# Weight load cut in two, first phase reordered, early x load, and state transposed by the DMA in a fused cross-attention and gated-FFN kernel

## The chip, the cores and the metric

One core of a Trainium2 chip runs the whole program. The metric is the device time of one launch in microseconds (us), lower is better. Each kernel ran on the same chip as the kernel before, in alternating rounds, and "faster" or "slower" needs 2%. A variant and the changed kernel mostly ran on different chips. Some executions list a mean granted TensorE clock of 0.985 to 0.993 instead of 0.997 to 1.0. By the medians most kernels took 0.4 to 2 us longer in them (state_pe did not); the experiments give the median of the full-clock executions as well, and where it matters the text says which kind a profile was.

Names: PE is TensorE (matmuls), DVE is VectorE, ACT is ScalarE, POOL is GpSimd, SP is the engine that only issues DMAs ("SPq" is its queue).

## The reference

There are 8 batches of `x` (8 heads, 512 rows, 64 columns) and of `state` (8 heads, 32 rows, 64 columns). Attention is read both ways between them; the two results, 544 rows of 512 columns per batch, go through a gated feed-forward layer with 1536 hidden columns.

```python
scores = scale * np.matmul(x, state.transpose(0, 1, 3, 2))     # scale = 1/8
a = softmax(scores)                                            # over the 32 state rows
xread = np.matmul(a, state)                                    # 512 rows
scores2 = scale * np.matmul(state, x.transpose(0, 1, 3, 2))
sread = np.matmul(softmax(scores2), x)                         # 32 rows
x = np.concatenate([xread, sread], axis=2)                     # heads side by side: 512 columns
gate = np.maximum(x @ w_gate, 0.0)
val = x @ w_val
out = gate * val @ w_out
```

Inputs and outputs are fp32; the kernel computes in bf16.

## The kernel before

The kernel never forms `xread`. It multiplies the state of a batch into the weights first (U = state @ w, small matmuls of 64 rows by 32 columns), then multiplies U by the attention. Four matmuls of 512 columns make a gate/value group (128 hidden columns of one batch), four more an output piece.

The order of everything is by hand. A list, `FIRST`, holds batches 0 and 1 and the start of batch 2; a loop does the rest. Each engine takes its instructions strictly in the order in which the list names them. These steps matter here:

```python
def w_dma(lo, hi, after=None):          # ("w", lo, hi): columns lo..hi of both weights, issued by GpSimd
    for w, src in enumerate((moe_w_gate, moe_w_val)):
        d = nc.gpsimd.dma_start(out=wsb[w][:, :, lo:hi], ...)
        loads["gv"[w], lo] = d.ins.name
        gate(d, after)

def x_dma(b, lo=0, n=H, after=None):    # ("xl", b, head, heads, gate): x of batch b, issued by SP
    d = nc.sync.dma_start(out=xf[b][:, lo:lo + n], in_=x_rows(b, lo, n))
    gate(d, after)                      # after = a load that must have landed first

def st_mm(b0, n):                       # state of n batches transposed by PE: 4 matmuls per batch
    ps = ps_st[b0] = ...
    for k in range(n):
        for par in range(2):
            for half in range(2):
                nc.tensor.matmul(ps[64 * half:64 * half + 64, k], st_b[:, b0 + k, par],
                                 perm[:, par, half]...)

# "u": U piece (columns lo..lo+n);  "ue": its eviction;  "g": gate/value group;  "om": output piece
# "conv": fp32 x to bf16;  "xt", "xe": x transposed by PE, evicted (batches 0 and 1)
# "x_bar": x transposed by the DMA (batch 2 on);  "sc": scores;  "at", "ae": attention transposed, evicted
# "dummy": matmuls on zeros that keep PE busy in stretches that wait
```

The weight stream of the first phase is `("w", 0, 256)`, `("w", 256, 512)`, `("w", 512, 1024)`, `("w", 1024, 1536)`, then three loads of `w_out`. x of batch 2 is held back until the last value columns have landed: `("xl", 2, 0, 8, ("v", 1024))`. States 2 to 7 come in one load, are cast on VectorE and transposed by 24 PE matmuls.

The softmax here doesn't subtract the row's maximum and nothing guards it: scores larger than these inputs give would overflow.

Of the kernel before, what the change touches and what calls it, by code (L numbers as in the profile page):

```python
# [8 lines left out]
FP32 = mybir.dt.float32  # L9
BF16 = mybir.dt.bfloat16  # L10
# [5 lines left out]

FIRST = [
    ("dummy", 9), ("w", 0, 256, ("s", 0)), ("st_cast", 0, 1, "v"), ("st_mm", 0, 1), ("st", 1, 2),
    ("xl", 1, 0, 2, ("x", 0, 4)), ("xl", 1, 2, 2), ("xl", 1, 4, 2), ("xl", 1, 6, 2), ("dummy", 2),
    ("st_ev", 0, 1, "a"), ("conv", 0, 0, 2, "v"), ("xt", 0, 0), ("dummy", 1), ("conv", 0, 2, 2, "v"),  # L20
    ("xe", 0, 0, "a"), ("xt", 0, 1), ("sc", 0, 0, (0,)), ("conv", 0, 4, 2, "v"), ("xe", 0, 1, "a"), ("dummy", 2),
    ("xt", 0, 2), ("exp", 0, 0, 0, 1), ("conv", 0, 6, 2, "v"), ("sc", 0, 0, (1,)), ("dummy", 2), ("xe", 0, 2, "a"),
    ("st_cast", 1, 2, "v"), ("xt", 0, 3), ("sum", 0, 0, 0, 1), ("st_mm", 1, 1), ("exp", 0, 0, 1, 1),
    ("sc", 0, 1, (0,)), ("xe", 0, 3, "a"), ("dummy", 3), ("sum", 0, 0, 1, 1), ("mul", 0, 0, 0, 1, "p"),
    ("st_ev", 1, 1, "a"), ("sc", 0, 1, (1,)), ("dummy", 2), ("w", 256, 512, ("g", 0)), ("exp", 0, 1, 1, 1),
    ("mul", 0, 0, 1, 1, "v"), ("u", 0, 0, 256), ("exp", 0, 1, 0, 1), ("sum", 0, 1, 1, 1), ("u", 1, 0, 256),
    ("ue", 0, 0, 256, 1, "a"), ("sr", 0), ("sum", 0, 1, 0, 1), ("ue", 1, 0, 256, 1, "a"), ("dummy", 4),
    ("conv", 1, 0, 2, "p"), ("ue", 0, 0, 256, 0, "a"), ("mul", 0, 1, 1, 1, "v"), ("mul", 0, 1, 0, 1, "p"),
    ("xt", 1, 0), ("sre", 0), ("dummy", 2), ("ue", 1, 0, 256, 0, "a"), ("conv", 1, 2, 2, "p"), ("at", 0, 0),
    ("conv", 1, 4, 2, "v"), ("at", 0, 1), ("xe", 1, 0, "a"), ("ae", 0, 0, "v"), ("w", 512, 1024), ("xt", 1, 2),  # L30
    ("xt", 1, 1), ("ae", 0, 1, "a"), ("xe", 1, 2, "v"), ("sc", 1, 0, (0,)), ("dummy", 1), ("xe", 1, 1, "v"),
    ("exp", 1, 0, 0, 1), ("sc", 1, 1, (0,)), ("g", 0, 1), ("exp", 1, 1, 0, 1), ("conv", 1, 6, 2, "v"),
    ("w", 1024, 1536), ("gr", 0, 1), ("sum", 1, 1, 0, 1), ("xt", 1, 3), ("sc", 1, 0, (1,)), ("dummy", 4),
    ("xe", 1, 3, "a"), ("gm", 0, 1), ("exp", 1, 0, 1, 1), ("sc", 1, 1, (1,)), ("mul", 1, 1, 0, 1, "p"),
    ("sum", 1, 0, 0, 1), ("exp", 1, 1, 1, 1), ("u", 0, 256, 256), ("wo", 0, 4), ("u", 1, 256, 256),
    ("ue", 0, 256, 256, 0, "a"), ("sum", 1, 1, 1, 1), ("g", 0, 0), ("ue", 0, 256, 256, 1, "a"),
    ("mul", 1, 0, 0, 1, "p"), ("sum", 1, 0, 1, 1), ("gr", 0, 0), ("g", 0, 2), ("mul", 1, 1, 1, 1, "p"),
    ("ue", 1, 256, 256, 1, "v"), ("ue", 1, 256, 256, 0, "a"), ("mul", 1, 0, 1, 1, "p"), ("dummy", 1), ("gm", 0, 0),
    ("gr", 0, 2), ("g", 0, 3), ("wo", 4, 8), ("gm", 0, 2), ("gr", 0, 3), ("at", 1, 1), ("wo", 8, 12), ("at", 1, 0),
    ("gm", 0, 3), ("ae", 1, 1, "a"), ("sr", 1), ("ae", 1, 0, "a"), ("u", 0, 512, 256), ("sre", 1), ("u", 0, 768, 256),  # L40
    ("ue", 0, 512, 256, 0, "a"), ("ue", 0, 512, 256, 1, "v"), ("g", 1, 1), ("ue", 0, 768, 256, 0, "a"),
    ("ue", 0, 768, 256, 1, "v"), ("g", 0, 5), ("gr", 1, 1), ("gr", 0, 5), ("gm", 1, 1), ("g", 0, 6), ("gm", 0, 5),
    ("gr", 0, 6), ("g", 0, 7), ("gm", 0, 6), ("xl", 2, 0, 8, ("v", 1024)), ("gr", 0, 7), ("st", 2, 8), ("g", 1, 3),
    ("gm", 0, 7), ("gr", 1, 3), ("u", 0, 1280, 256), ("gm", 1, 3), ("g", 0, 4), ("ue", 0, 1280, 256, 0, "a"),
    ("gr", 0, 4), ("ue", 0, 1280, 256, 1, "v"), ("g", 1, 2), ("gm", 0, 4), ("gr", 1, 2), ("u", 0, 1024, 256),
    ("g", 0, 11), ("gm", 1, 2), ("ue", 0, 1024, 256, 0, "a"), ("gr", 0, 11), ("ue", 0, 1024, 256, 1, "v"),
    ("g", 0, 10), ("gm", 0, 11), ("gr", 0, 10), ("g", 0, 8), ("gm", 0, 10), ("gr", 0, 8), ("g", 0, 9), ("gm", 0, 8),
    ("gr", 0, 9), ("u", 1, 1024, 256), ("g", 1, 0), ("gm", 0, 9), ("ue", 1, 1024, 256, 1, "a"),
    ("ue", 1, 1024, 256, 0, "a"), ("u", 1, 512, 256), ("gr", 1, 0), ("om",), ("ue", 1, 512, 256, 0, "v"),
    ("ue", 1, 512, 256, 1, "a"), ("gm", 1, 0), ("g", 1, 9), ("gr", 1, 9), ("g", 1, 8), ("gm", 1, 9), ("gr", 1, 8),  # L50
    ("u", 1, 1280, 256), ("om",), ("gm", 1, 8), ("ue", 1, 1280, 256, 1, "a"), ("ue", 1, 1280, 256, 0, "a"),
    ("xb_alloc", 2), ("conv", 2, 0, 4, "v"), ("conv", 2, 4, 4, "p"), ("om",), ("g", 1, 11), ("xc", 2, 0, 2, "v"),
    ("xc", 2, 2, 2, "p"), ("at_alloc", 2), ("x_bar", 2), ("xl", 3, 0, 8), ("oe",), ("st_cast", 2, 8, "v"),
    ("gr", 1, 11), ("g", 1, 10), ("gm", 1, 11), ("gr", 1, 10), ("st_mm", 6, 2), ("gm", 1, 10), ("st_mm", 4, 2),
    ("st_ev", 6, 2, "a"), ("st_mm", 2, 2), ("st_ev", 4, 2, "v"), ("u", 1, 768, 256), ("st_ev", 2, 2, "a"), ("om",),
    ("ue", 1, 768, 256, 1, "v"), ("ue", 1, 768, 256, 0, "a"), ("u_alloc", 2), ("u", 2, 512, 512),
    ("ue", 2, 512, 512, 0, "a"), ("ue", 2, 512, 512, 1, "v"), ("sc", 2, 1), ("sc", 2, 0), ("ue", 2, 512, 512, 3, "a"),
    ("om",), ("ue", 2, 512, 512, 2, "v"), ("exp", 2, 1), ("om",), ("exp", 2, 0), ("sum", 2, 1), ("u", 2, 1024, 512),
    ("xb_alloc", 3), ("conv", 3, 4, 4, "p"), ("oe",), ("ue", 2, 1024, 512, 0, "a"), ("sr", 2),
    ("ue", 2, 1024, 512, 3, "a"), ("om",), ("mul", 2, 1, 0, 2, "p"), ("sum", 2, 0), ("ue", 2, 1024, 512, 2, "a"),  # L60
    ("om",), ("sre", 2), ("mul", 2, 0, 0, 2, "p"), ("ue", 2, 1024, 512, 1, "a"), ("conv", 3, 0, 4, "v"), ("g", 1, 7),
    ("a_bar", 2), ("xc", 3, 0, 2, "v"), ("xc", 3, 2, 2, "p"), ("at_alloc", 3), ("x_bar", 3), ("xl", 4), ("gr", 1, 7),
    ("g", 1, 6), ("gm", 1, 7), ("gr", 1, 6), ("g", 1, 5), ("gm", 1, 6), ("gr", 1, 5), ("g", 1, 4), ("gm", 1, 5),
    ("gr", 1, 4), ("om",), ("gm", 1, 4), ("u", 2, 0, 512), ("oe",), ("ue", 2, 0, 512, 0, "v"), ("om",),
    ("ue", 2, 0, 512, 2, "a"), ("ue", 2, 0, 512, 1, "v"), ("ue", 2, 0, 512, 3, "a"), ("om",), ("om",), ("oe",),
]

@with_exitstack
def kernel(
# [9 lines left out]
    nc = tc.nc  # L79

    B, H, S, D = x.shape
# [8 lines left out]
    def pool(name, bufs, space=None):  # L90
        if space is None:
            return ctx.enter_context(tc.tile_pool(name=name, bufs=bufs))
        return ctx.enter_context(tc.tile_pool(name=name, bufs=bufs, space=space))

    const = pool("const", 1)
# [14 lines left out]
    id128 = const.tile([128, 128], BF16, name="id128")  # L110
    perm = const.tile([128, 2, 2, NJ, 64], BF16, name="perm")
    xs_all = [const.tile([128, NC, NJ, 132], BF16, name="xs%d" % i) for i in range(3)]
    warm = const.tile([128, 512], BF16, name="warm")
    st_f = const.tile([128, B, 2, D], FP32, name="st_f")
    st_b = const.tile([128, B, 2, D], BF16, name="st_b")
    stT = const.tile([128, B, NJ, 64], BF16, name="stT")
    brT = const.tile([128, B, NJ * Ns], BF16, name="brT")
    tiny = const.tile([128, 1], FP32, name="tiny")
# [4 lines left out]
    def cp(eng, o, i):  # L123
        if eng == "a":
            nc.scalar.copy(out=o, in_=i)  # L125
        elif eng == "v":
            nc.vector.tensor_copy(out=o, in_=i)  # L127
        else:
            nc.gpsimd.tensor_copy(out=o, in_=i)  # L129
# [4 lines left out]
    def gate(d, after):  # L134
        if after is not None:
            info = mybir.DependencyInfo(mybir.DependencyClass.Sync, mybir.DependencyReason.DATA)
            tc.add_manual_dep(d.ins, loads[after], info, reason="order of loads")

    def st_dma(lo, hi, after=None):
        src = state.rearrange("b h (m t) d -> (h m) b (t d)", t=2)[:, lo:hi]  # L140
        d = nc.sync.dma_start(out=st_f[:, lo:hi].rearrange("p b t d -> p b (t d)"), in_=src)
        loads["s", lo] = d.ins.name
        gate(d, after)

# [42 lines left out]

    def st_ev(b0, n, eng):
        cp(eng, stT[:, b0:b0 + n].rearrange("p b j c -> p (b j c)"), ps_st[b0].rearrange("p b c -> p (b c)"))



# [262 lines left out]

    nc.vector.memset(warm, 0.0)  # L456
    make_identity(nc, id128)
    st_dma(0, 1)
    for j in range(NJ):
        x_dma(0, 2 * j, 2)  # L460
# [5 lines left out]
    for i in range(3):  # L466
        set_ones(i)

    steps = {
        "dummy": dummies, "w": w_dma, "wo": wo_dma, "st": st_dma,  # L470
        "st_cast": st_cast, "st_mm": st_mm, "st_ev": st_ev, "conv": x_conv, "xc": x_copy, "xt": x_tr, "xe": x_ev,
        "sc": sc_mm, "exp": sc_exp, "sum": nrm_sum, "mul": nrm_mul, "at": a_tr, "ae": a_ev,
        "u": u_mm, "ue": u_ev, "g": gv_mm, "gr": gv_relu, "gm": gv_mult, "gv": gv, "om": out_mm, "oe": out_ev, "sr": sr_mm, "sre": sr_ev, "out": outp,
        "xb_alloc": xb_alloc, "at_alloc": at_alloc, "u_alloc": u_alloc, "x_bar": x_bar, "a_bar": a_bar, "ub": u_burst, "xl": x_dma,
# [94 lines left out]
```

## Time and profile before

| | |
|---|---|
| time | 227.07 us (median of 3, 226.51 to 227.14) |
| span in the profile | 224.4 us |
| PE busy | 96% of the span |
| PE's one long wait | 1.78 us, ends at 22.65 us, on value weights 512 to 1023 |
| from 22.65 us to the first gate/value group of batch 2 (57.68 us) | 35.03 us |
| from there to the end of the span | 166.7 us |

The head of the page names each engine's busy time, its share of the span and its instruction count:

```profile
span 224.4 us, 4881 instructions
...
PE 214.4 (96%) x1947; PEld 106.1 (47%) x1969; DVE 140.0 (62%) x246; ACT 117.3 (52%) x218; POOL 37.2 (17%) x47
```

PE is 96% busy in 224.4 us, so the kernel can become shorter only by a few waits at the start or by less PE work. The prediction below shows where these are. SP's timeline (start, duration of the issue, instruction) shows when x of batch 2 was asked for, and when its transpose was:

```profile
27.32 0.38 SPq L151 DMA_DIRECT2D xf<-in_x_dram  x1
...
40.02 1.35 SPq L238 DMA_TRANSPOSE xT<-xb  x1
```

By the tile's view the transpose needed 4.8 us to land, so it was there at 44.8 us, and the scores of batch 2 that read it started at 45.15 us. The slack of that chain was about 0.3 us. The last value weights landed at 27.3 us (the x load is held for them and went out at 27.32) and PE asked for them at 27.52 us: a slack of 0.2 us.

VectorE's timeline shows the same conversion of x (two heads, fp32 to bf16) at two prices. The first is of batch 0, with GpSimd idle; the second of batch 1, with GpSimd converting and issuing a load next to it:

```profile
4.95 0.43 DVE L127 CAST xs<-xf 128x512 bf16<-128x512 f32 x1
...
12.33 0.81 DVE L127 CAST xs<-xf 128x512 bf16<-128x512 f32 x1 [0.70 <-DMA xf<-in_x_dram]
```

### The profile page before, as it was taken

The numbers are of one execution on the slowest core, as the hardware profiler recorded it, in microseconds if no ns is written. First come the engines' busy times: TensorE is split into PE (matmuls) and PEld (weight loads), VectorE is DVE, ScalarE is ACT, GpSimd is POOL, SyncE is SP. The second block draws the span as 40 slices with busy tenths as digits, with TensorE's granted clock in tenths as the row PEclk, the third lists the DMA queues.
The fourth block names the chain that finished last, engine by engine and source line by source line (L and its number), as shares of the span: only waits on it lengthen the run. The fifth ranks groups of instructions, "written<-read, shape, count | busy, mean of one in ns | idle before, by whom it ended". The sixth has DMA issues, their size and how long they took to land.

```text
span 224.4 us, 4881 instructions
## 1 busy us (share of the span) xinstructions
PE 214.4 (96%) x1947; PEld 106.1 (47%) x1969; DVE 140.0 (62%) x246; ACT 117.3 (52%) x218; POOL 37.2 (17%) x47
## 2 busy tenths in 40 slices
PE   6887999999999999999999999999999999999994
PEld 3553444444544444444444444444444444586543
DVE  4777796888377657866595659564956544452210
ACT  3787777676373646363745465455636344343111
POOL 4496001225070160007000700000000000000000
PEclk9999999999999999999999999999999999999999
DMA  6999998674944851385119611361131111111133
GB/s 181 262 201 206 204 226 238 112 265 79 218 183 101 243 132 47 67 267 134 55 33 283 121 47 50 93 146 50 47 93 57 47 47 50 47 48 38 59 80 107
DMA packets 40551, 27.84 MB, mean 124 GB/s; under 512 B 21200, under 2 KB 36304, under 8 KB 40528
## 3 DMA queue, kind: packets, MB, share of 16 engines
q1 hardware_dynamic: 34720, 22.81, 36.6%
q0 software_dynamic: 5808, 4.72, 13.6%
q8 instruction: 15, 0.25, 0.5%
q14 instruction: 8, 0.07, 0.1%
HBM read 18.35 MB, written 8.91 MB: 121 GB/s over the span
## 4 chain that ended last, share of the span: by engine, by line
PE 88%; DMA 6%; POOL 2%; SPq 1%; issue 1%; DVE 0%; ACT 0%; POOLq 0%
PE o_ps L400 38%; PE gv_ps L363 36%; PE u_ps L311 5%; PE gvs_ps L385 5%; DMA wv_sb<-in_moe_w_val_dram 4%; DMA st_f<-in_state_dram 2%; PE sc_ps L246 1%; PE o_ps L425 1%; PE sr_ps L292 1%; SPq L151 1%; POOL wg_sb L157 1%; PE stT_ps L184 1%; POOL xs L129 1%; POOL a_sn L269 1%; POOL wv_sb L157 0%
## 5 line engine op out<-in xcount | busy, mean ns | idle before, releaser
L372 DVE TENSOR_TENSOR h_sb<-gv_ps,g_sb 128x512 bf16<-128x512 f32 x96 | 65.5, 689 | 48.7 <-ACT g_sb L369 48.2
L363 PE MATMUL gv_ps<-ans,U 128*128 128x512 bf16 x384 | 94.3, 379 | 0.1
L400 PE MATMUL o_ps<-wo_sb,h_sb 128*128 128x512 bf16 x350 | 91.3, 379 | 1.4 <-issue 0.5
L369 ACT ACTIVATE g_sb<-gv_ps 128x512 bf16<-128x512 f32 x96 | 57.4, 598 | 55.1 <-PE gv_ps L363 54.3
L363 PEld LDWEIGHTS <-U 128*128 128x128 bf16 x384 | 36.4, 98 | 42.5 <-issue 1.0
L400 PEld LDWEIGHTS <-h_sb 128*128 128x128 bf16 x372 | 35.1, 98 | 43.1 <-issue 4.2
L125 ACT CAST U<-u_ps 128x512 bf16<-128x512 f32 x55 | 29.2, 596 | 5.1 <-PE u_ps L311 4.5
L127 DVE CAST U<-u_ps 128x512 bf16<-128x512 f32 x41 | 25.7, 673 | 3.7 <-PE u_ps L311 3.5
L129 POOL CAST xb<-xf 128x1024 bf16<-128x1024 f32 x10 | 10.2, 1043 | 83.8 <-PE gv_ps L363 38.2
L125 ACT COPY o_sb<-o_ps 128x512 f32<-128x512 f32 (+2 forms) x20 | 10.8, 538 | 19.2 <-PE o_ps L400 17.5
L127 DVE COPY o_sb<-o_ps 128x512 f32<-128x512 f32 (+2 forms) x18 | 11.4, 636 | 9.9 <-ACT o_sb L125 4.5
L257 ACT ACTIVATE e_sn<-sc_ps 128x512 bf16<-128x512 f32 (+1 forms) x20 | 10.1, 514 | 9.9 <-PE sc_ps L246 9.7
L311 PE MATMUL u_ps<-wv_sb,stT 64*32 64x256 bf16 (+1 forms) x280 | 9.6, 309 | 2.2 <-DMA wv_sb<-in_moe_w_val_dram 2.2
L389 DVE TENSOR_TENSOR hs_sb<-gvs_ps,g_sb 128x256 bf16<-128x256 f32 x12 | 5.1, 424 | 9.9 <-ACT g_sb L388 9.9
L263 DVE TENSOR_REDUCE cs<-e_sn 128x8 f32<-128x256 bf16 (+2 forms) x15 | 10.6, 708 | 0.5 <-ACT e_sn L257 0.3
L129 POOL COPY xs<-xb 128x1024 bf16<-128x1024 bf16 x10 | 10.4, 1065 | 1.0 <-DVE xb L127 0.7
L311 PEld LDWEIGHTS <-stT 64*32 64x32 bf16 x560 | 5.9, 90 | 9.8 <-issue 8.0
L311 PE MATMUL u_ps<-wg_sb,stT 64*32 64x256 bf16 (+1 forms) x280 | 10.0, 315 | 0.0
L388 ACT ACTIVATE g_sb<-gvs_ps 128x256 bf16<-128x256 f32 x12 | 4.6, 384 | 10.2 <-PE gvs_ps L385 7.8
L454 PE MATMUL warm_ps<-warm 128*128 128x256 bf16 x33 | 6.7, 321 | 1.2 <-DVE warm L456 1.2
L246 PEld LDWEIGHTS <-xT 128*128 128x128 bf16 x128 | 5.8, 98 | 4.2 <-ACT xT L125 0.7
L246 PE MATMUL sc_ps<-stT,xT 128*128 128x64 bf16 x128 | 6.9, 193 | 0.4
(48 smaller groups left out, 109.6 us busy)
## 6 DMA issues: line engine op xcount, KB each, us to landing
out_dram<-o_sb SPq DMA_DIRECT2D x31, 256.0 KB, 2.4
xf<-in_x_dram SPq DMA_DIRECT2D x6, 1024.0 KB, 6.7
xf<-in_x_dram SPq DMA_DIRECT2D x8, 256.0 KB, 4.8
wo_sb<-in_moe_w_out_dram POOLq DMA_DIRECT2D x3, 512.0 KB, 14.1
wg_sb<-in_moe_w_gate_dram POOLq DMA_DIRECT2D x2, 512.0 KB, 8.0
wv_sb<-in_moe_w_val_dram POOLq DMA_DIRECT2D x2, 512.0 KB, 10.6
wg_sb<-in_moe_w_gate_dram POOLq DMA_DIRECT2D x2, 256.0 KB, 5.4
wv_sb<-in_moe_w_val_dram POOLq DMA_DIRECT2D x2, 256.0 KB, 5.8
```

The lines of the kernel that those rows point to most:

```text
L125: nc.scalar.copy(out=o, in_=i)
L127: nc.vector.tensor_copy(out=o, in_=i)
L129: nc.gpsimd.tensor_copy(out=o, in_=i)
L246: nc.tensor.matmul(ps_sc[b, kc][:, c, :, j2], xT[b][:, c, j], stT[:, b, j].rearrange("p (s n) -> p s n", s=2), start=True, stop=True)
L257: nc.scalar.activation(out=esl(e_sn, b, kc, j2, n).rearrange("p k j n -> p k (j n)"), in_=ps_sc[b, kc].rearrange("p c s j n -> p (c s) j n ...
L263: nc.vector.reduce_sum(out=c, in_=e, axis=AX.X)
L311: nc.tensor.matmul(ps[32 * j:32 * j + 32, 0:n], stT[r, b, j, 32 * kc:32 * kc + 32], wsb[w][r, j, lo:lo + n], start=(i == 0), stop=True, sk ...
L363: nc.tensor.matmul(ps.rearrange("p (c t) -> p c t", c=NC), U[b][:, kc, w, f0:f0 + 128], ANS[b][:, :, kc], start=(kc == 0), stop=(kc == 1))
L369: nc.scalar.activation(out=g_sbs[b, jf], in_=ps_g[b, jf][0], func=AF.Relu)
L372: nc.vector.tensor_tensor(out=hsb[b][:, jf], in0=ps_g[b, jf][1], in1=g_sbs[b, jf], op=ALU.mult)
L385: nc.tensor.matmul(ps[:, w].rearrange("p (b n) -> p b n", b=B), wsb[w][:, j, f0:f0 + 128], brT[:, :, 32 * j:32 * j + 32], start=(j == 0), ...
L400: nc.tensor.matmul(o_ps[0], src[:, jf, t0:t0 + 128], wo_sb[:, jf], start=(jf == 0), stop=(jf == NF - 1))
```

## The change

The intent: let PE work through the arrival of the weights without the 1.78 us wait, and take the state transposes of batches 3 to 7 off PE. Its four parts, cut to their core:

```diff
 FIRST = [                                    # (reordered throughout; only the marked steps here)
-    ("w", 512, 1024)                         # after the evictions of batch 0's attention
+    ("w", 512, 768)                          # right behind ("w", 256, 512)
+    ("w", 768, 1024)
-    ("xl", 2, 0, 8, ("v", 1024))             # x of batch 2 held for the last value weights
+    ("xl", 2, 0, 8, ("v", 768))              # ... for columns 768 to 1023
-    ("st", 2, 8), ("st_cast", 2, 8, "v"), ("st_mm", 6, 2), ("st_mm", 4, 2), ("st_mm", 2, 2)
+    ("st", 2, 3), ("st_cast", 2, 3, "v"), ("st_mm", 2, 1)
+    ("st", 3, 8), ("st_z", 0, "p"), ("st_z", 1, "v"), ("st_z", 3, "v"), ("st_z", 2, "a"), ("st_bar",)
 ]
+    sz_f = const.tile([128, B - 3, 2, D], FP32, name="sz_f")
+    sz_b = const.tile([128, B - 3, 2, 2, D], BF16, name="sz_b")
...
+    def st_z(r, eng):
+        p = slice(32 * r, 32 * r + 32)
+        cp(eng, sz_b[p, :, :, r % 2], sz_f[p])
+
+    def st_bar():
+        nc.sync.dma_start_transpose(out=stT[:, 3:B].rearrange("p b (g j) c -> p (b g) (j c)", g=2),
+                                    in_=sz_b.rearrange("p b g s d -> p (b g s d)"))
...
+    nc.gpsimd.memset(sz_b, 0.0)
```

`st_z` copies 32 rows of one head into the half of a zeroed tile that this head owns, so that one DMA transpose ("the crossbar") gives the layout that the PE matmuls gave before. The gate/value order is the part that the short diff cannot show. Ahead of the first U piece from the last weight columns (1280 to 1535) the list before has nine gate/value groups; the changed list has twelve, because it takes the work of *both* batches on the columns that are there before it asks for new ones:

```text
before:   (0,1) (0,0) (0,2) (0,3) (1,1) (0,5) (0,6) (0,7) (1,3)                     then U of columns 1280
changed:  (0,1) (0,0) (0,3) (0,2) (0,5) (1,1) (1,0) (0,4) (1,4) (1,5) (0,7) (0,6)   then U of columns 1280
          (batch, group of 128 columns)
```

## The prediction

> **What bounds the kernel now.** I read the slices of the page first, then PE's timeline, then what PE waited for.
>
> ```profile
> PE   6887999999999999999999999999999999999994
> DMA  6999998674944851385119611361131111111133
> ```
>
> One digit is a fortieth of 224.4 us, so 5.6 us. From the fifth slice on PE (TensorE) is full to the end; in slices 2 to 6 the DMA engines are full too. So only the first 23 us or so are not bound by PE's own work: there the weights arrive. The list of PE's waits agrees:
>
> ```profile
> PE u_ps L311 <- DMA wv_sb<-in_moe_w_val_dram: 2.2, 2, 1.8
> ...
> PE o_ps L400 <- issue: 0.5, 3, 0.2
> ```
>
> The long wait is in PE's timeline (start, duration, instruction, count):
>
> ```profile
> 18.79 1.03 PE L363 MATMUL gv_ps<-ans,U 128*128 128x512 bf16 x4
> 19.66 0.61 PE L274 MATMUL aT_ps<-id,a_sn 128*128 128x128 bf16 x8
> 20.20 0.43 PE L292 MATMUL sr_ps<-xs,e_sn 128*32 128x65 bf16 x32
> 20.56 0.30 PE L311 MATMUL u_ps<-wg_sb,stT 64*32 64x256 bf16 x8
> 22.65 0.30 PE L311 MATMUL u_ps<-wv_sb,stT 64*32 64x256 bf16 x8 [1.78 <-DMA wv_sb<-in_moe_w_val_dram]
> 22.76 0.30 PE L311 MATMUL u_ps<-wg_sb,stT 64*32 64x256 bf16 x8
> 22.86 0.30 PE L311 MATMUL u_ps<-wv_sb,stT 64*32 64x256 bf16 x8
> 23.10 4.49 PE L363 MATMUL gv_ps<-ans,U 128*128 128x512 bf16 x20
> 27.52 0.30 PE L311 MATMUL u_ps<-wg_sb,stT 64*32 64x256 bf16 x8
> 27.64 0.29 PE L311 MATMUL u_ps<-wv_sb,stT 64*32 64x256 bf16 x8
> 27.87 1.90 PE L363 MATMUL gv_ps<-ans,U 128*128 128x512 bf16 x8
> ...
> 41.85 1.50 PE L184 MATMUL stT_ps<-perm,st_b 128*64 128x256 bf16 x24
> 43.28 0.30 PE L311 MATMUL u_ps<-wg_sb,stT 64*32 64x256 bf16 x8
> ```
>
> What to see: at 20.56 the order demands U from columns 512 to 767, but they come in one load of 512 columns and land at 22.65, though gate and value work of batch 1 on columns 0 to 511 was ready to run. From 22.65 PE never stops again. Whatever changes the end must bring useful PE work before that point, or take PE work away after it.
>
> Unit costs, from differences of starts, since durations overlap: a gate/value or output group of four 512-column matmuls 0.8625 us (16 of them from 50.11 to 53.56 is 3.45). Eight U matmuls of 256 columns 0.11 us, so a 256-column U piece (16) 0.22, a 512-column one 0.43. From 23.10 to 27.87 there are 20 x 0.2156 = 4.31 of full matmuls and one U piece of 0.22; 0.24 is left over, the price of going into the 64*32 mode and out again. The 24 state matmuls take 43.28 - 41.85 = 1.43.
>
> **What the Trainium skill says.** "TensorEngine Tiling (Array Packing)", section Key Properties: changing the tiling mode drains TensorE. The trace agrees: about 0.12 us a switch, by the sum above. "DMA: Bandwidth & Descriptors", section Queues, rings and completion order: each DMA engine goes round robin between the queue rows that have work, packet by packet. The trace agrees in kind: in stretches of 2 us the weight queue moved 0.40 to 0.41 MB alone (16 to 24 us), but 0.32, 0.24 and 0.16 MB from 30, 32 and 34 us, while the x queue took 0.13, 0.24 and 0.42. The same page, section DMA Transpose (X-bar), lets 2-byte data be transposed by the DMA from SP: here an xT transpose of sixteen 128x128 blocks lands in 4.5 us (median).
>
> **The change part by part.** Both first phases hold 24 gate/value groups, 15 U pieces and 12 output pieces; the loop behind is unchanged. So I compare the start of batch 2's gate/value work: 57.68 us before.
>
> *Earlier stream.* The load of columns 512 to 1023 is cut in two, and 512 to 767 is issued right behind 256 to 511. The stream was already busy, so bytes do not come faster: columns to 1023 landed at 22.6, those to 511 at about 15.6, so 767 should land near 19. GpSimd pays two more issues at 0.77 us. Its queue, by durations of before: first multiply ends about 8.8; four issues to 11.9; convert 0.65, multiply 0.63, convert 0.65 to 13.8; four issues to 16.9; two multiplies of 512 columns at 1.34 (2.69 for two at 50.13) to 19.6.
>
> *New order of PE.* The last x pair of batch 1 is converted at 13.8; transpose, copy, scores put gate/value (0,1) at about 15.0 (14.23 before). Then 0.86, U 0.46, state read 0.4, three groups 2.6: 19.4; U of columns 512 is then there. The transposes of batch 1's attention wait for the multiply at 19.6; with the state matmuls of batch 2 (0.24) and another U piece, gate/value (0,5) starts at about 21.0. My estimate from single durations.
>
> *What is left from there.* 20 gate/value 17.25; 12 output 10.35; seven 256-column U 1.54; three 512-column U 1.29; scores of batch 2 0.48; state read 0.36; nine excursions into other modes at 0.235, 2.1. Sum 33.4, so 54.4. The same sum for before from 22.65: rest of the U pieces 0.45, 17.25, 10.35, six U 1.32, three 1.29, state matmuls 1.43, 0.36, 0.48, nine excursions 2.1, two switches inside an excursion 0.24: 35.3, against 35.03 seen. So the account holds to 0.3.
>
> 57.68 - 54.4 gives 3.3 us: 1.65 from starting 1.65 earlier (21.0 for 22.65) and the rest, some 1.65, from less work. Of that, state matmuls are 1.43: 20 fewer in all, about 1.2, and four that moved ahead. The count of mode switches hardly falls (33 changes of mode in the new first phase, 32 in the old): I give that part of the title almost nothing.
>
> *Off the path.* The crossbar for states 3 to 7 replaces PE work, a 1.40 us VectorE cast and three copies of 0.6 to 0.7 by four row copies and ten transposed blocks (estimate from 4.5 us for sixteen: 3 us). It is needed only by scores of batch 3, at about 56. Four more dummy matmuls lie in stretches that wait anyway. The memset of the padded state lies in GpSimd's idle time of 1.60 us before the first weights.
>
> **The rivals.** (1) *The early x load delays the weights.* x of batch 2 is now released by columns 768 to 1023 (about 22.6) and not by the last columns (27.3). The last weights landed at 27.3 without it. In the trace x of batch 2, issued at 27.3, moved little before 30 and needed 10.9 us. Issued at 22.6 it would take from about 25 on a fifth to a third of the stream and put the last columns at 28.5 to 29.9 (estimate from the 2 us stretches). PE wants them at 21.0 + 3.45 + 0.46 + 1.73 + 0.46 + 1.73 = 28.8. So a wait of 0 to 1 us, mean perhaps 0.4: a gain of 2.9, or 2.3 at the bad end. (2) *The front is slower than I think.* GpSimd's chain carries more issues; each 0.3 us of slip in a multiply or conversion goes straight to PE. 0.3 to 1 us more lost. (3) *The state's copies block an in-order engine.* The load of states 3 to 7 is queued on SP behind the x transposes of batch 2, so goes out at about 36 and lands near 42 (estimate); VectorE reaches its copies at about 42.5. A late landing stops VectorE and then, PSUM full, PE. There is about 2 us of slack in PSUM buffers, so I expect nothing; badly, 2 us and a gain of 1. (4) *Output weights late.* x takes from their stream too, but the total of bytes until 38 us is no larger; third output piece at about 39.4. Nothing. (5) *More gain than the sum:* only if PE's front end starts before 21.0; the x and weight landings leave at most half a microsecond: 4 us in all.
>
> **Range and chances.** 3.3 from the sum, less 0.4 for the shared stream and a further 0.1 for slips: 2.8 us. The time is then 227.07 - 2.8 = 224.3. The good end is 4 us and a bit (222.8), the bad end rivals 1 to 3 together (226.2). The line for faster is 222.5, 4.5 us: beyond what the account offers, 0.08. Slower than 231.6 needs a broken tail: 0.02. Within 2%: 0.90.
>
> **What would show it.** Right: PE's wait for the value weights before columns 512 gone; gate/value (0,5) of batch 0 near 21.0; batch 2's gate/value starts near 54.5 to 55; the state group of 24 gone from the timeline; the steady loop unchanged to 0.3 us. Wrong: a wait of over 1 us at the U piece of columns 1280 (rival 1), PE idle before the attention transposes at 19 to 21 (rival 2), VectorE idle on the state load near 42 (rival 3), or a wait of scores of batch 3 for a transpose. If batch 2 starts at 54.5 and the end does not follow, my claim that the rest is unchanged is wrong.

## The result

The changed kernel took 224.77 us (median of 4 runs, 224.15 to 225.06); the kernel before, in the same rounds, 227.10 us (226.51 to 228.21). A ratio in this document is the mean time of one kernel's runs over that of the other's of the same rounds, so not quite the ratio of the medians: here 0.9888, with a 95% interval of 0.9845 to 0.9932. That is 1.1% faster, "same" by the 2% line. Outputs are correct.

The page of the changed kernel, head and two rows of the slices (one digit is a fortieth of the span, in tenths busy):

```profile
span 222.4 us, 4870 instructions
...
PE 215.7 (97%) x1953; PEld 105.2 (47%) x1953; DVE 141.1 (63%) x245; ACT 114.4 (51%) x212; POOL 41.8 (19%) x51
...
PE   6979999999999999999999999999999999999994
...
DMA  6999998979936831576138811351131111111133
```

PE is full one slice sooner: the seven in the fourth slice before (16.8 to 22.4 us) is a nine. (PE's busy time rises by 1.3 us although it has less to do. Matmul records can be missing from a trace; the steady loop's output matmuls count 372 after and 350 before for the same work. So I compare starts of instructions, not busy sums.)

PE's waits (engine, line, releaser: total us, times, longest):

```profile
PE xT_ps L246 <- DVE xs L128: 1.3, 3, 0.6
...
PE xT_ps L246 <- POOL xs L130: 0.6, 1, 0.6
...
PE sc_ps L260 <- DMA xT<-xb: 0.2, 1, 0.2
```

No wait for weights is left. In its place stand waits for *conversions of x* in the first 14 us, and a small one for a transposed x much later. PE's timeline shows where (start, duration, instruction, count, idle time before it):

```profile
12.77 0.40 PE L246 MATMUL xT_ps<-id,xs 128*128 128x128 bf16 x4 [0.61 <-POOL xs L130]
13.65 0.40 PE L246 MATMUL xT_ps<-id,xs 128*128 128x128 bf16 x4 [0.49 <-DVE xs L128]
...
14.80 0.39 PE L246 MATMUL xT_ps<-id,xs 128*128 128x128 bf16 x4
...
15.84 1.03 PE L377 MATMUL gv_ps<-ans,U 128*128 128x512 bf16 x4
...
20.24 0.30 PE L325 MATMUL u_ps<-wg_sb,stT 64*32 64x256 bf16 x8
20.36 0.29 PE L325 MATMUL u_ps<-wv_sb,stT 64*32 64x256 bf16 x8
...
21.82 3.63 PE L377 MATMUL gv_ps<-ans,U 128*128 128x512 bf16 x16
...
29.72 0.30 PE L325 MATMUL u_ps<-wg_sb,stT 64*32 64x256 bf16 x8
29.84 0.29 PE L325 MATMUL u_ps<-wv_sb,stT 64*32 64x256 bf16 x8
...
55.38 1.04 PE L377 MATMUL gv_ps<-ans,U 128*128 128x512 bf16 x4
...
57.43 0.41 PE L260 MATMUL sc_ps<-stT,xT 128*128 128x64 bf16 x8 [0.15 <-DMA xT<-xb]
```

Read it from the top. U of columns 512 (20.24, 20.36) runs without a pause, since value columns 512 to 767 landed at 19.3 us. Group (0,5) of batch 0 starts at 21.82. U of the last columns (29.72, 29.84) runs without a pause too: these weights landed at 28.3 us. Batch 2 starts at 55.38, 2.30 us sooner than before. At 57.43 the scores of batch 3 wait 0.15 us for a transposed x. The rest of the span takes 222.4 - 55.38 = 167.0 us, against 166.7 before: that is unchanged to 0.3.

The conversions behind the first two waits, in VectorE's timeline:

```profile
6.94 0.43 DVE L128 CAST xs<-xf 128x512 bf16<-128x512 f32 x1 [0.48 <-DMA xf<-in_x_dram]
...
12.43 1.16 DVE L128 CAST xs<-xf 128x512 bf16<-128x512 f32 x1 [0.51 <-DMA xf<-in_x_dram]
```

The same instruction takes 0.43 us for batch 0 and 1.16 us for batch 1, where GpSimd runs a conversion (12.06 to 12.71), a multiply (12.64 to 13.30) and another conversion (13.21 to 14.06).

How x of batch 2 shares the DMA engines is seen in two stretches of 2 us, 22 to 24 and 30 to 32 us (queue: packets, MB, share; q0 is the weight queue, q1 that of SP with x):

```profile
q0 software_dynamic: 374, 0.37, 111.0%
q1 hardware_dynamic: 160, 0.03, 14.3%
...
q0 software_dynamic: 242, 0.24, 70.0%
q1 hardware_dynamic: 242, 0.25, 45.2%
```

x was asked for at 21.99 us and hardly moved at first (its queue took 0.03 MB from 22 to 24); from 26 us on it took half of the bytes. It landed at 35.6 us, 13.6 us after it was asked for and 2.6 us sooner than before (38.2).

### The profile page after: what moved, and what is told of

It is laid out like the page before. It is cut to its first block, busy times and chain, and to the rows that moved or that the text cites. A ratio compares the mean times of both kernels' runs of the same rounds, so it can differ in the third digit from the quotient of the medians.

```text
span 222.4 us, 4870 instructions
## 1 busy us (share of the span) xinstructions
PE 215.7 (97%) x1953; PEld 105.2 (47%) x1953; DVE 141.1 (63%) x245; ACT 114.4 (51%) x212; POOL 41.8 (19%) x51
## 4 chain that ended last, share of the span: by engine, by line
PE 89%; DMA 7%; DVE 1%; SPq 1%; issue 0%; ACT 0%
PE o_ps L414 38%; PE gv_ps L377 37%; PE u_ps L325 6%; PE gvs_ps L399 5%; DMA xf<-in_x_dram 4%; DMA xT<-xb 2%; PE sc_ps L260 1%; PE o_ps L439 1%; PE sr_ps L306 1%; SPq L156 1%; PE aT_ps L288 1%; DVE xs L128 1%; DVE U L128 0%; DVE ans L128 0%; SPq L142 0%
## 5 line engine op out<-in xcount | busy, mean ns | idle before, releaser
L414 PE MATMUL o_ps<-wo_sb,h_sb 128*128 128x512 bf16 x372 | 94.1, 379 | 0.0
L383 ACT ACTIVATE g_sb<-gv_ps 128x512 bf16<-128x512 f32 x96 | 57.3, 597 | 54.5 <-PE gv_ps L377 53.9
L126 ACT CAST U<-u_ps 128x512 bf16<-128x512 f32 x52 | 27.7, 595 | 5.8 <-PE u_ps L325 5.2
L128 DVE CAST U<-u_ps 128x512 bf16<-128x512 f32 x44 | 27.7, 674 | 0.8 <-PE u_ps L325 0.8
L130 POOL CAST xb<-xf 128x1024 bf16<-128x1024 f32 x11 | 11.2, 1040 | 71.3 <-DMA xf<-in_x_dram 71.3
L130 POOL COPY xs<-xb 128x1024 bf16<-128x1024 bf16 x11 | 11.2, 1042 | 1.0 <-DVE xb L128 0.7
L277 DVE TENSOR_REDUCE cs<-e_sn 128x32 f32<-128x1024 bf16 (+2 forms) x13 | 10.4, 801 | 0.4 <-ACT e_sn L271 0.2
```

The source lines that it names most:

```text
L126: nc.scalar.copy(out=o, in_=i)
L128: nc.vector.tensor_copy(out=o, in_=i)
L130: nc.gpsimd.tensor_copy(out=o, in_=i)
L277: nc.vector.reduce_sum(out=c, in_=e, axis=AX.X)
L383: nc.scalar.activation(out=g_sbs[b, jf], in_=ps_g[b, jf][0], func=AF.Relu)
L414: nc.tensor.matmul(o_ps[0], src[:, jf, t0:t0 + 128], wo_sb[:, jf], start=(jf == 0), stop=(jf == NF - 1))
```

## The experiments

Twelve runs in three calls; the kernel before ran in each (medians 226.99, 227.57 and 227.08 us). All kernels gave correct results.

| run | what it is | time (us) | ratio to before | 95% | full-clock runs: median (of 6) | before, the same |
|---|---|---|---|---|---|---|
| changed_again | the changed kernel, unaltered | 224.58 | 0.9880 | 0.9842 to 0.9918 | 224.56 (5) | 227.15 |
| one_load | changed, columns 512 to 1023 in one load | 225.54 | 0.9919 | 0.9874 to 0.9964 | 225.23 (4) | 226.97 |
| unpaired | changed, nine groups ahead of columns 1280 | 225.18 | 0.9899 | 0.9874 to 0.9925 | 225.19 (6) | 227.06 |
| x_late | changed, x of batch 2 behind the last weights | 228.05 | 1.0025 | 0.9976 to 1.0075 | 227.84 (1) | 226.97 |
| state_pe | changed, states 3 to 7 by PE | 227.01 | 0.9979 | 0.9938 to 1.0021 | 227.20 (5) | 226.97 |
| state_pe2 | the same, with the memset kept | 226.02 | 0.9954 | 0.9917 to 0.9991 | 225.78 (5) | 227.06 |
| warm | changed, nine more dummies | 225.01 | 0.9883 | 0.9849 to 0.9917 | 225.01 (6) | 227.15 |
| conv_act | changed, one x conversion on ScalarE | 226.04 | 0.9952 | 0.9920 to 0.9984 | 225.60 (5) | 227.06 |
| b_split_move | before, load split, one U piece moved | 227.11 | 1.0003 | 0.9953 to 1.0053 | 226.97 (5) | 226.97 |
| b_front | the same, mended | 227.65 | 0.9996 | 0.9963 to 1.0029 | 227.50 (5) | 227.15 |
| b_xbar | before, with the crossbar alone | 227.99 | 1.0048 | 1.0004 to 1.0091 | 227.36 (3) | 227.06 |
| b_front_xbar | before, with both | 228.30 | 1.0013 | 0.9974 to 1.0053 | 228.21 (5) | 227.15 |

The ratios and their intervals use all executions. Three of the profiles are at 0.992, and in each the low clock is one stretch of some 4 us, with 1.00 around it, that begins at or just behind PE's waits for data: in conv_act the mean granted clock is 0.83, 0.50 and 0.81 in 8 to 10, 10 to 12 and 12 to 14 us (waits of 0.77 and 0.84 us just before), in b_front 0.96, 0.50 and 0.68 in 10 to 12, 12 to 14 and 14 to 16 us (waits of 0.82 and 1.09 us), in b_front_xbar 0.50 and 0.66 in 30 to 32 and 32 to 34 us (a wait of 2.16 us).

My theory: 1.7 us of the gain is the wait at 22.65 us, 1.3 us is PE work that went to the crossbar, each worth its amount alone. The rival: the parts depend on each other, and one of them alone gives little, since something else binds just behind.

### Taking one part out of the changed kernel

**one_load.** The load of columns 512 to 1023 is joined again.

```diff
-    ("w", 512, 768), ...  ("w", 768, 1024), ...  ("xl", 2, 0, 8, ("v", 768)),
+    ("w", 512, 1024), ...                        ("xl", 2, 0, 8, ("v", 512)),
```

> The changed kernel, but columns 512 to 1023 of both weights in one load each again, issued where the load of 512 to 767 is, and x of batch 2 released by it. My theory (the split is what lets PE go on at 20.2 us): the U piece of columns 512 waits for the whole load, until about 22.0 where columns 768 to 1023 landed in the changed kernel, so a wait of 1.5 to 1.8 us comes back at that piece and the time is 226.3 to 226.6. Rival (the bytes are the same and only the order of the work matters; the split is worth nothing): no wait there, 224.8 within 0.4.

Measured 225.54 us. The wait came back where it had been:

```profile
21.82 0.30 PE L325 MATMUL u_ps<-wv_sb,stT 64*32 64x256 bf16 x8 [1.01 <-DMA wv_sb<-in_moe_w_val_dram]
```

It is 1.0 us and not the 1.5 to 1.8 I expected, and the time lies between the two expectations: some 0.8 us above the changed kernel, which is not clear of noise (the intervals overlap). The profile is clearer: from gate/value (0,1) to (0,5) it took 7.35 us (15.94 to 23.29) against 5.98 in both profiles of the changed kernel. So the split takes 1.4 us off PE's path in this order.

**unpaired.** The changed kernel with nine gate/value groups ahead of the last columns instead of twelve, so the old way of asking for new columns early. The groups and U pieces behind stand in another order too; the loads, the states and x are as in the changed kernel.

```diff
-    ... ("g", 1, 5), ("u", 1, 768, 256), ("g", 0, 7), ("g", 0, 6), ("u", 0, 1280, 256), ...
+    ... ("u", 0, 1280, 256), ("g", 0, 7), ("g", 0, 6), ("g", 1, 5), ...     (evictions moved along)
```

> The changed kernel, but the U piece of columns 1280 is asked for after one group of batch 1 on columns 512 to 1023 and not after four gate/value groups and a U piece more; those groups come later. Theory (the gain of the new order is that both batches' work on the columns at hand lies before the demand for the next; the stream is the bound up to 28.3): demand at about 26.5, the last columns land at 28.3 to 28.6, so a wait of 1.6 to 2.1 and 226.2 to 226.9. Rival (once the load is split, any order of these groups does): no wait over 0.3, 224.6 to 225.

Measured 225.18 us. The wait for the last weights is there:

```profile
28.55 0.30 PE L325 MATMUL u_ps<-wv_sb,stT 64*32 64x256 bf16 x8 [1.13 <-DMA wv_sb<-in_moe_w_val_dram]
```

Its direction is as expected, its size half. From (0,5) to batch 2 it took 34.55 us instead of 33.23 (changed_again). The time rose by 0.4 to 0.6 us only, because in this profile (0,5) started 0.2 us sooner and the tail behind batch 2's start was 166.6 us instead of 167.1. A difference of that size is not clear of noise, so what this run shows is the wait in its trace: the order of twelve groups is what hides the late landing of the last weights.

**x_late.** x of batch 2 held for the last weights, as before the change.

```diff
-    ("xl", 2, 0, 8, ("v", 768)),
+    ("xl", 2, 0, 8, ("v", 1024)),
```

> The changed kernel, but x of batch 2 released by the last weight columns again (about 28 us for 22). My theory (the early x load is no gain in itself but the new order, which has taken batch 2's scores forward, needs it): x lands near 38.5 in place of 35.6, its two conversions end near 40.6, the transposed x comes near 46, PE waits 2 to 4 us around the first scores of batch 2 at 42.9: 227 to 228.5. Rival (it only shares the stream, so without it the weights come sooner and nothing waits): 224.8 within 0.4 or a little faster.

Measured 228.05 us: the whole gain is gone, as expected. x was asked for at 28.02 us and landed 10.9 us later at 38.9, 3.3 us after the changed kernel's; its transpose was asked for at 41.04 and needed 5.2 us; PE stood:

```profile
46.33 0.41 PE L260 MATMUL sc_ps<-stT,xT 128*128 128x64 bf16 x8 [1.64 <-DMA xT<-xb]
```

From (0,5) to batch 2 it took 35.92 us, 2.7 more than in changed_again; most of what the wait leaves of that is in two sets of U pieces that were held by evictions (1.30 and 1.09 us for what took 0.85). Five of the six executions were at the lower clock, so the loss in the table has some of that in it; the one at full clock took 227.84 us. In the new order PE asks for the scores of batch 2 at 42.88 us; the transposed x of the changed kernel lands at 37.73 + 5.0 = 42.7.

**state_pe and state_pe2.** States 3 to 7 loaded, cast and transposed by 20 PE matmuls again, at the place where the changed list has them ready. state_pe drops the memset too; state_pe2 keeps one of the same bytes, since the first profile had a slow start.

```diff
-    ("st_z", 0, "p"), ("st_z", 1, "v"), ... ("st_z", 3, "v"), ... ("st_z", 2, "a"), ... ("st_bar",),
+    ("st_cast", 3, 8, "v"), ... ("st_mm", 3, 2), ("st_mm", 5, 2), ("st_mm", 7, 1), ("st_ev", 3, 2, "a"), ...
-    nc.gpsimd.memset(sz_b, 0.0)
+    nc.gpsimd.memset(pad, 0.0)       # twice; in state_pe2 alone
```

> The changed kernel, but states 3 to 7 are transposed by PE again: one cast by VectorE and 20 state matmuls in one excursion after the output pieces at about 51.4 us, no crossbar. My theory (PE never rests there, so its work is time): 20 times 0.06 plus one excursion of 0.24 is 1.4, less at most 0.2 that PE now waits for the transposed x of batch 3: 226.0 to 226.2. Rival (the crossbar and its copies cost about what they save, through waits of VectorE and a busy transpose queue): 224.8 within 0.4.

> States 3 to 7 by PE in the changed order, as before, but with GpSimd's early memset kept at its old cost (two of 640 columns on an unused buffer), so that the front is that of the changed kernel. From gate/value (0,5) to batch 2's gate/value took 33.2 to 33.6 us in the changed kernel's two profiles and 34.55 in the first try. Theory (the state work costs PE 1.3 and the crossbar gives back up to 0.6; the rest of the first try's 2.4 was a slower front, by luck of the load of x or by the missing memset): that stretch 34.3 to 34.6 again, time 225.5 to 226.3. Rival (PE state work costs the full 2.4): 226.8 to 227.3 with a front no later than the changed kernel's 22.5.

state_pe measured 227.01 us, more than I expected. Its profile has (0,5) at 23.60 us; the profiled front was 1.1 us later than that of changed_again (22.48), with half-rate matmuls and a late load of x. state_pe2 measured 226.02 us, inside its expectation and 1.25 to 1.44 us above the changed kernel (224.77, 224.58). In both, (0,5) to batch 2 takes 34.55 us, 1.32 more than in changed_again, and here is the difference:

```profile
52.74 1.28 PE L188 MATMUL stT_ps<-perm,st_b 128*64 128x256 bf16 x20
```

It runs from 52.74 to the next group at 53.95: 1.21 us, as the prediction had it (1.2 for 20). So in the new order the crossbar gives about its full PE time in this stretch: 1.32 us against changed_again, 1.0 against the first profile of the changed kernel (33.56). The front stays open: in state_pe2's profile too (0,5) came late, at 23.33 us, although the memset was kept. In both, a conversion of batch 1's x on VectorE took 1.5 to 1.6 us beside GpSimd's work.

### Adding one part to the kernel before

**b_split_move.** The load is split, and U of columns 768 goes behind two groups that don't need it.

```diff
-    ("w", 512, 1024),
+    ("w", 512, 768), ("w", 768, 1024),
-    ("u", 0, 512, 256), ("u", 0, 768, 256), ... ("g", 1, 1), ("g", 0, 5), ...
+    ("u", 0, 512, 256), ... ("g", 1, 1), ("g", 0, 5), ("u", 0, 768, 256), ...
```

> The kernel before, with only the load of columns 512 to 1023 cut in two at its old place, and the U piece of columns 768 moved behind gate/value (1,1) and (0,5). State on PE and late x as before. My theory (the wait of 1.8 us at 20.6 is a matter of which columns are asked for): U of columns 512 goes at about 20.6, the two gate/value groups fill the time to 22.6, the wait falls to under 0.3: 225.3 to 225.6. Rival (the new order of the whole front is what removes it, and with the old order GpSimd's two more issues push the multiplies back): 226.5 to 227.5.

Measured 227.11 us, ratio 1.0003: a miss. No wait for weights stands at 20.6 us any more. Two new ones do:

```profile
21.03 0.62 PE L274 MATMUL aT_ps<-id,a_sn 128*128 128x128 bf16 x8 [0.73 <-POOL a_sn L269]
```

One is for a multiply on GpSimd, which now stands behind two more load issues of 0.75 to 0.8 us each; the other, 0.68 us at 25.49, for the eviction of a U piece that is used right after it is made. This is my edit's fault, not the old order's, so I mended it.

**b_front.** As b_split_move, with the first `w_out` issue behind the four multiplies and one more group ahead of the use of the late U piece.

```diff
-    ("u", 0, 256, 256), ("wo", 0, 4), ... ("mul", 1, 0, 1, 1, "p"), ("dummy", 1), ...
+    ("u", 0, 256, 256), ... ("mul", 1, 0, 1, 1, "p"), ("wo", 0, 4), ("dummy", 1), ...
+    ... ("g", 0, 5), ("u", 0, 768, 256), ("g", 1, 3), ("g", 0, 6), ("g", 0, 7), ("u", 0, 1280, 256), ...
```

> The kernel before with the load of columns 512 to 1023 cut in two, the U piece of columns 768 behind gate/value (1,1) and (0,5), gate/value (1,3) behind it to cover its eviction, and the first output weights issued after the four multiplies on GpSimd. Theory (the earlier try failed only through two waits that it made itself, 0.7 for a multiply and 0.7 for an eviction): the 1.8 us wait is gone and not replaced, 225.2 to 225.8. Rival (what bounds the front is GpSimd's queue, so the two issues of 0.77 us come out as PE's wait again): 226.5 to 227.

Measured 227.65 us, ratio 0.9996: a second miss. The two waits for columns 512 and 768 are gone and nothing was gained. At the last columns the weights now bind:

```profile
29.12 0.30 PE L311 MATMUL u_ps<-wv_sb,stT 64*32 64x256 bf16 x8 [0.62 <-DMA wv_sb<-in_moe_w_val_dram]
```

(This profile is an execution at 0.992 and had 1.9 us of waits for the *first* weights, at 10 to 11.4 us; so its absolute times are not to be compared. The five full-clock executions, 227.50 us, show no gain either.) The slack of 0.2 us that the profile before showed at this point is the reason that I give: with the same nine groups ahead, time saved earlier only makes PE ask sooner for weights that have not landed. b_front_xbar, below, shows just that. But the weights were later as well: in this profile the last ones landed at 29.1 us, with their last issue on GpSimd at 17.66 us (27.3 and 15.07 in the kernel before), and in the other three profiles of the old order at 28.1 to 29.2. How much of this comes from the two more issues and how much changes from run to run is not separated.

**b_xbar.** The kernel before with the crossbar for states 3 to 7, and nothing else (state load split in two, `st_z`, `st_bar` and the memset as in the change).

```diff
-    ("st", 2, 8), ... ("st_cast", 2, 8, "v"), ... ("st_mm", 6, 2), ("st_mm", 4, 2), ("st_mm", 2, 2), ...
+    ("st", 2, 3), ("st", 3, 8), ... ("st_cast", 2, 3, "v"), ("st_z", 0, "p"), ("st_z", 1, "v"), ...
+    ("st_z", 3, "v"), ("st_mm", 2, 1), ("st_z", 2, "a"), ("st_bar",), ...
```

> The kernel before with only states 3 to 7 by the crossbar. Theory (PE work is time): 20 state matmuls fewer, 1.2, less up to 0.6 for new waits on the transposed data: 226.0 to 226.8 against 227.1 to 227.6. Rival (the old order asks for the transposed x and attention just when they come, so the crossbar's extra transpose in the same queue delays them and eats it all): 227 to 228, with waits of scores or gate/value of batch 2 for a transpose, as the 0.5 and 0.6 us in the run with the mended front.

Measured 227.99 us, ratio 1.0048 with an interval just above 1. Half of its executions were at the lower clock; the three others have 227.36 us against 227.06. So I read it as no faster, and leave open whether it is slower. The rival holds. Two waits stand in its profile:

```profile
28.21 0.30 PE L327 MATMUL u_ps<-wv_sb,stT 64*32 64x256 bf16 x8 [1.04 <-DMA wv_sb<-in_moe_w_val_dram]
...
45.74 0.64 PE L262 MATMUL sc_ps<-stT,xT 128*128 128x64 bf16 x16 [0.81 <-DMA xT<-xb]
```

The first has nothing to do with the crossbar: the front of this run was quicker (PE asked at 26.88 instead of 27.52) and the weights were not. The second stands where the state matmuls are gone: PE reaches the scores of batch 2 before the transposed x does. The scores of batch 3 wait another 0.50 us for a transposed x at 61.00 us, and the tail behind batch 2's start takes 167.6 us instead of 166.7. From the gate/value group behind this U piece to batch 2's start it took 58.61 - 28.45 = 30.16 us, and in the kernel before 57.68 - 27.87 = 29.81.

**b_front_xbar.** Both of these together on the old order.

> The same, with states 3 to 7 by the crossbar from masked rows. Theory (PE's state matmuls are time, the crossbar is off the path): 20 times 0.06 less, so 1.0 to 1.3 below the run without it: 224.1 to 224.6, at or a little below the changed kernel with the old order of the front. Rival (crossbar and copies bring waits of their own, as the 0.3 for transposed x and 0.3 for PSUM in the changed kernel's trace): 0.3 to 0.7 below it only.

Measured 228.30 us, ratio 1.0013: the third miss of this kind. PE asked for the last value weights at 26.81 us, 0.7 us sooner than in the kernel before, and waited 2.16 us for them, then 0.58 us for a transposed attention and 0.5 us for a transposed x:

```profile
29.27 0.30 PE L327 MATMUL u_ps<-wv_sb,stT 64*32 64x256 bf16 x8 [2.16 <-DMA wv_sb<-in_moe_w_val_dram]
```

This profile is one at 0.992, the slowest of its six, and its low clock cost more: the next two groups took 3.1 us instead of 1.8. The five full-clock executions have 228.21 us against 227.15, so they show no gain either. What I expected from the two parts together, some 3 us, is found as waits.

### Trying to better the changed kernel

**changed_again** is the changed kernel, so that the next kernels have it in their own call.

> The changed kernel unaltered, beside the others of this call. In the last call the same front (PE's work up to gate/value (0,5)) ended at 21.8 us in one profile of it, but 22.95 to 23.6 in two variants that don't touch the front, where the second x pair of batch 0 came 0.3 to 1.4 us later and PE's small matmuls took 0.61 us a group for 0.40. My theory (arrival of x differs from run to run, and with it the front): 224.3 to 225.5, with single runs up to 227. Rival (the state in PE form really changes the front): every run of this one within 0.5 of 224.8.

Measured 224.58 us, ratio 0.9880: the gain repeats. Its profile has (0,5) at 22.48 and batch 2 at 55.71 us, so 33.23 us between them:

```profile
22.48 3.63 PE L377 MATMUL gv_ps<-ans,U 128*128 128x512 bf16 x16
...
55.71 1.04 PE L377 MATMUL gv_ps<-ans,U 128*128 128x512 bf16 x4
```

**warm.** In changed_again's profile the first transposes of x ran at a lower rate:

```profile
6.12 0.61 PE L246 MATMUL xT_ps<-id,xs 128*128 128x128 bf16 x4 [0.75 <-DVE xs L128]
```

A group of four took 0.61 us there and 0.40 in the first profile of the same kernel. Three numbers of dummies were raised to fill PE's gaps.

```diff
-    ("dummy", 3), ... ("dummy", 1), ... ("dummy", 2),
+    ("dummy", 6), ... ("dummy", 5), ... ("dummy", 4),
```

> The changed kernel with nine more dummy matmuls before the second, third and fourth x pairs of batch 0 are there. Theory (PE falls to half rate when it rests for x at 5 to 6.5 us, and the dummies keep it from that): no group of four transposes longer than 0.42 us, the slow runs vanish, median 0 to 0.6 below the unaltered kernel. Rival (dummies only stand in the way): 0.3 to 0.9 slower than it, as each takes 0.11.

Measured 225.01 us against 224.58 and 224.77: no gain. All transposes took 0.40 us, yet (0,5) started at 23.09 us, since PE waited 1.03 us for VectorE's conversion of batch 1's x, which took 1.74 us here. In this profile a full rate from the start did not make the front earlier; the conversions bound it. One profile can't say that the dummies cured the slow rate, as it comes and goes without them.

**conv_act.** The conversion that took 1.16 us on VectorE is put on ScalarE.

```diff
-    ("conv", 1, 4, 2, "v"), ("mul", 0, 1, 1, 1, "p"), ("xe", 1, 0, "a"), ("xt", 1, 1), ...
+    ("mul", 0, 1, 1, 1, "p"), ("xe", 1, 0, "a"), ("conv", 1, 4, 2, "a"), ("xt", 1, 1), ...
```

> The changed kernel with the third conversion of batch 1's x (1.16 us on VectorE beside GpSimd's casts) on ScalarE. Theory (the front runs at the pace of those conversions, PE waits 0.5 to 0.8 for it before the transposes of the third pair): the wait shrinks, gate/value (0,5) starts 0.2 to 0.4 earlier, 224.3 to 224.6; the gain may be lost again where scores of batch 3 already wait for the transposed x. Rival (ScalarE's copies are then the pace): 224.6 to 225.2.

Measured 226.04 us: slower than the changed kernel by 1.3 to 1.5 us, and by 1.0 with full-clock executions alone (225.60 to 224.56). PE waited 0.86 us for ScalarE's conversion, which stands in its order behind an eviction. (The profiled execution is the one at 0.992, so its front is late for that reason too: (0,5) at 24.30 us.) From (0,5) to batch 2 it took 33.23 us, as in changed_again; another 1.04 us was lost at 130.62 us, in the steady loop, where scores waited for a transposed x. The move brought no gain; why the full-clock executions are slower is open, and the run does not tell what made VectorE's conversion slow. No version that I ran beats the changed kernel.

## Why the prediction was right

The time (224.77 us for 224.3) and the class were right, and the range held it. Step by step:

- **Earlier stream: right.** Columns to 767 landed at 19.3 us ("near 19"), those to 1023 at 22.0, and the wait at 20.6 us is gone.
- **New order of PE: late by 0.8 us, and this is the term that was mis-sized.** Gate/value (0,1) came at 15.84 us instead of "about 15.0", and (0,5) at 21.82 instead of "about 21.0"; from one to the other 5.98 us passed, and the prediction had 6.0. So all of the slip lies ahead of (0,1). I had followed GpSimd's chain alone, with its conversions of batch 1's x at their undisturbed cost, and let the last one end at 13.8. It ended at 14.06: 0.26 us. The rest is VectorE's conversion of the third pair, which is not in the sum. It took 1.16 us and ended at 13.59; PE waited 0.61 us for GpSimd's conversion and 0.49 us for this one, and scores and eight attention transposes that stand behind it in PE's order kept the transposes of the last pair until 14.80, 0.74 us after their x was there. The profile before had this in view: the same conversion beside GpSimd's work took 0.81 us there. That GpSimd's work causes it is read from the overlap, but the overlap is firm. In the 14 kept profiles VectorE's timeline lists 75 of these conversions of two heads one by one: the 38 beside an idle GpSimd took 0.43 us each, the 17 beside a conversion or multiply of GpSimd 0.48 to 1.74 us, and the 20 beside load issues alone 0.41 to 0.72 us. The one run that moved the conversion didn't settle it. The Trainium skill, "SBUF — State Buffer", section Who interferes with whom, would explain it (a cast of VectorE that uses both ports, and GpSimd, lock each other out for an instruction), and the timeline fits: 1.16 us is about the rest of GpSimd's conversion and multiply (12.43 to 13.2) plus 0.43. No run here tests this mechanism.
- **What is left from there: right.** 33.4 us predicted; 33.56 and 33.23 measured in two profiles of the kernel, and 35.03 before. The saving of 1.5 to 1.8 us is the predicted 1.65. state_pe2 confirms its larger part: 34.55 - 33.23 = 1.32 us (1.0 against the first profile) for the 20 state matmuls and the switches around them.
- **Batch 2's start:** 55.38 us for 54.4 by the sum and 54.5 to 55 with slips. The gain is 2.30 us for 3.3 by the sum and 2.8 after the deductions. Of the missing 1.0 us, 0.82 is the front, and 0.16 lies in the stretch.
- **Off the path: right in result, with less margin than I thought.** The state load went out at 39.13 us, not at about 36, because x of batch 2 landed later than I took it to; it landed at 44.9, not near 42. VectorE stood 1.34 us and ScalarE 0.91 us for it. In the first profile three U pieces at 48.62 to 49.67 us took 1.05 us instead of the 0.77 of state_pe, so PE lost about 0.3; in changed_again it lost nothing there.
- **Rival 1 (x delays the weights): it cost nothing, and that x delays them is hardly shown.** The last weights landed at 28.3 us, 1.0 us later than before, just below my 28.5 to 29.9 (29.0 in changed_again). But in x_late, where x goes out behind them, they landed at 28.0 us, and in four profiles of the old order at 28.1 to 29.2. So at most some of the 1.0 us is x's doing. x took half of the bytes and not "a fifth to a third", but hardly moved before 26 us. The slower front meant that PE asked at 29.72 us, not 28.8. So the 0.4 us set aside for this rival was spent by rival 2: that the number came so near is partly luck. With the order unpaired the wait does appear (1.13 us).
- **Rival 2 (slower front): this is what happened.** Rival 3 showed in idle engines and hardly in PE; rivals 4 and 5 not at all.
- **The tail follows the start of batch 2, as claimed**: 166.7 us before, 167.0 after, 167.1 in changed_again. In the first profile of the changed kernel the extra 0.3 is the small wait of batch 3's scores at 57.43 us, a case which the prediction named only among its signs.
- **Mode switches:** the account with 0.12 us a switch holds to 0.3 us for both kernels, and the number of changes (33 and 32) is no gain. No run changed this number alone, so that part is only argued.

What the prediction did not contain, and the runs showed: **the parts don't add up one by one.** It counts 1.65 us for the earlier start and 1.65 us for less work as if each stood alone. Alone, in the old order, the first is worth nothing (b_front, ratio 0.9996) and neither is the second (b_xbar, 1.0048). The kernel before had, in its profile, three things within 0.3 us of each other: PE, the last weights (slack 0.2) and the transposed x of batch 2 (slack 0.3). Whoever makes PE quicker there meets one of the other two, as the waits of b_xbar and b_front_xbar show. The changed kernel moves all three: the list of twelve groups asks later for the last weights, the early x load brings the transposed x forward by some 2 us (44.8 to 42.7), and only then do the split load and the crossbar give PE time that counts. One step is left open: I did not run the old order with an early x load alone or with the crossbar, so how much that load would give there is not known. Nor is it known how much of the waits in those runs comes from last weights that landed 0.8 to 1.9 us later than in the profile of the kernel before.

## What to carry to other kernels

Before you credit a change with the wait or the work that it removes, look at each later point where the same engine takes over data from another, and write down the slack: the gain of a lone edit is cut off at the smallest one. In a phase that is bound by arriving data, one lever is the order of work: use up everything that the arrived data allows, for all batches, before asking for the next piece. And take the cost of a conversion from a place in the trace where its neighbours are as busy as they will be in the changed kernel.

## What the Trainium skill lacked or had wrong

- "TensorEngine Tiling (Array Packing)", Key Properties: says that a mode switch drains TensorE, but gives no price. Here it is about 0.12 us each way between 128*128 and 64*32 matmuls, by differences of starts in both kernels.
- "DMA: Bandwidth & Descriptors", Queues, rings and completion order: round robin by packets, without a figure for what a newcomer gets. Here a 1 MB load issued into a full weight stream moved next to nothing for 3 to 4 us (0.03 MB from 22 to 24 us), then got half of the bytes (0.25 and 0.24 MB in 2 us); it took 13.6 us to land, against a median of 6.9 for the loads of this size.
- The same page, DMA Transpose (X-bar): no time from issue to landing (elsewhere the page has a bandwidth for transposes). In two profiles of the changed kernel ten 128x128 blocks took 3.6 and 3.8 us, sixteen 4.3 to 5.9 us.
- "TensorE: Matmul & The Clock Gate", Part 1: The HAM clock gate: says that the slow state at a start varies from run to run, and this agrees (four transposes 0.61 us in one profile of the changed kernel, 0.40 in another). But the granted clock in the profile read 1.00 in that stretch too (4 to 10 us), so that view does not show the slow state at a start; the durations do. (The page does warn that the clock events of a trace are not always reliable.) A later stretch of it, in conv_act, the view does show (0.50 in 10 to 12 us).
